# Holding the loads behind the fourth unit until the first 288 columns' low rank is copied

## The chip, the cores and the metric

The kernel runs on one core of one Trainium2 chip. A core has TensorE (PE, matmuls; its weight loads are listed apart as PEld), VectorE (DVE), ScalarE (ACT), GpSimd (POOL) and SyncE (SP), which issues the DMA transfers. The metric is the device time of one execution in microseconds, lower is better. Comparisons leave disturbed runs out.

## What is computed

Two parts, one behind the other. The first is a gated linear attention over 4 batches, 8 heads, 768 steps and head dimension 48:

```python
f = 1.0 / (1.0 + np.exp(-f_logit))
for t in range(S):
    state = f[:, :, t, :, None] * state + np.einsum('bhd,bhe->bhde', k[:, :, t], v[:, :, t])
    y[:, :, t] = np.einsum('bhd,bhde->bhe', q[:, :, t], state)
```

Its output, with the heads side by side, is x, 768 x 384 for each batch. The second part mixes along the steps with a low rank of 32 and then along the channels with two weights, 384 x 1536 and 1536 x 384:

```python
xt = x.transpose(0, 2, 1)
h = xt @ U @ V
u = x + h.transpose(0, 2, 1)
ch = np.maximum(u @ w_ch1, 0.0) @ w_ch2
return u + ch
```

The four parameters U, V, w_ch1 and w_ch2 arrive as 8-byte floating-point numbers and are converted on the chip to 4-byte ones.

## The kernel before

A *unit* is one batch and one pair of heads, so there are 16 units, and units 0 to 3 are batch 0. Units 0 to 3 are worked off first, with nothing beside them. Then the low rank of batch 0 is formed, first for the 288 columns of units 0 to 2 and then for the last 96, and the channel matmuls of batch 0 run while units 4 to 7 are worked off, and so on.

Operands of even units come into the tile `late`, those of odd units into `other`, one third each for f, k and q; v has three buffers of its own. So unit 5 takes the places of unit 3 in `other`, and v of unit 5 the buffer of unit 2. `load` issues them on SP, two DMAs (two heads) each for f, k and q and three for v:

```python
    def load(n, *names):

        b, hp = divmod(n, HP)
        for nm in names:
            if nm == "v":
                v_tiles[n] = three.tile([P, NBL, 2, D], F32, name="v_nat")
            for par in range(2):
                head = src[nm][b, 2 * hp + par]
        ...
                if nm == "v" or n < TURNED:
                    dst = v_tiles[n] if nm == "v" else nat[n % 2][nm]
                    nc.sync.dma_start(out=dst[:, :, par, 0:D], in_=head.rearrange("(c p) d -> p c d", p=P))
                    continue
```

A weight is taken in by two calls. `start` gives it a staging buffer and issues its DMA; `end` converts it: two instructions on ScalarE (L90, L91), three on VectorE, one on GpSimd (L95):

```python
        def start():
            raw = pool.tile([P, WP], U64, name="w_raw", bufs=RAW) if place is None else place()
            raw = T["raw"] = raw[0:rows, 0:n]
            dma.dma_start(out=shaped(raw), in_=w)

        def end():
            y = pool.tile([P, WP], U32, name="w_y")[0:rows, 0:n]
            r = pool.tile([P, WP], I32, name="w_r", bufs=3)[0:rows, 0:n]
            words = T["raw"].bitcast(U32).rearrange("p (n two) -> p n two", two=2)
            lo, hi = words[:, :, 0], words[:, :, 1]

            f = y.bitcast(F32)
            nc.scalar.activation(f, hi.bitcast(F32), AF.Abs)
            nc.scalar.activation(r, lo, AF.Copy, scale=2.0**-29)
            nc.vector.tensor_scalar(f, f, SMALLEST, LARGEST, ALU.max, ALU.min)
            nc.vector.tensor_scalar(y, y, 3, 0x3FFFFFFF, ALU.logical_shift_left, ALU.bitwise_and)
            nc.vector.scalar_tensor_tensor(y, hi, 0xC0000000, y, ALU.bitwise_and, ALU.bitwise_or)
            nc.gpsimd.tensor_tensor(dst.bitcast(I32), shaped(y.bitcast(I32)), shaped(r), ALU.add)

        return start, end


def ahead_by(n, loads):


    def call(i):
        if i + n < len(loads):
            loads[i + n][0]()
        loads[i][1]()

    return [lambda i=i: call(i) for i in range(len(loads))]
```

U and V (three pieces) and the later pieces are staged in a pool of four buffers (`w_raw`); the first six pieces of w_ch1 (128 of its 1536 columns each) in halves of `zw` tiles, which have another use only later:

```python
    spare = []

    def place():
        if not spare:
            t = zp.tile([P, NFC // 2, 2 * P], F32, name="zw").rearrange("p i t -> p (i t)").bitcast(U64)
            spare.extend([t[:, 0:WP], t[:, WP : 2 * WP]])
        return spare.pop(0)

    FIRST = 6
    weights += [
        take_in(w1[:, :, i * P : (i + 1) * P], w1_rows[:, :, i * P : (i + 1) * P], place if i < FIRST else None)
        for i in range(NFC)
    ]
```

The framework orders the instructions of TensorE, VectorE and ScalarE as the program has them (`manual_schedule`). The DMA issues of SP and the work of GpSimd are ordered by the framework itself; it adds all waits, for data and for places that are still being read.

The first four units, the loads for the next two, and the start of the mixer:

```python
        for n in range(HP):
            pieces = front(n, "keep", "keys") + rear(n - 1, "scan", "scores")
            pieces += [lambda: busy(3)] + rear(n, "kept") + front(n, "read_back", "queries")
            if n + 1 < HP:
                pieces += front(n + 1, "gates") + rear(n - 1, "read", "inner") + rear(n, "states")
            for piece in pieces:
                piece()
            if n < 2:
                load(n + 2, "v")
            if n == 1:


                for start, _ in weights[: early + 2]:
                    start()
            elif n > 1:
                load(n + 2, "f", "k", "q", "v")
        for start, _ in weights[early + 2 : early + FIRST]:
            start()


        loads = ahead_by(early + FIRST, weights)
        done, rest = slice(0, 2 * n * D), slice(2 * n * D, DM)
        pieces = rear(n, "states") + rear(n - 1, "read") + rear(n, "scan") + loads[:1] + rear(n, "scores")
        pieces += loads[1:2] + rear(n - 1, "inner") + rear(n, "read") + loads[2 : early + 1]
        for piece in pieces:
            piece()
        m = mixer(0)
        low_rank_of, added_up_of, mix_of = m.some
        low_rank_of(done)
        loads[early + 1]()
        for piece in rear(HP - 1, "inner"):
            piece()
        added_up_of(done)
        low_rank_of(rest)
        mix_of(done)
        added_up_of(rest)
        mix_of(rest)
        loads = loads[early + 2 :]

        start = m.before[3:5] + m.firsts[0:1] + m.before[5:]

        EARLY = 6
        second = chain(front(HP, "gates", "keep", "keys", "read_back", "queries"), steps(HP, 2 * HP + 1))
        for i, (_, piece) in enumerate(start + m.firsts[1:]):
            piece()
            if loads:
                loads.pop(0)()
            if i >= EARLY:
                next(second)()
        for f in loads:
            f()
```

The low rank of some columns ends with a copy on ScalarE (L213), on which the next matmul waits:

```python
        def low_rank_of(cols):
            pm = ps_big.tile([P, 2, 512], F32, name="ph", tag="big")[:, 0]
            for c in range(NCH):
                g = slice((c % NG) * R, (c % NG + 1) * R)
                nc.tensor.matmul(pm[g, cols], lhsT=U[:, c, :], rhs=x[:, c, cols],
                                 start=(c < NG), stop=(c >= NCH - NG))
            if not hs:
                for i in range(2):
                    hs[i] = two.tile([P, DM], F32, name="h", bufs=2)
            nc.scalar.copy(hs[0][:, cols], pm[:, cols])

        def added_up_of(cols):
            pm = ps_big.tile([P, 2, 512], F32, name="ph", tag="big")[:, 0]
            nc.tensor.matmul(pm[:, cols], lhsT=blocks, rhs=hs[0][:, cols], start=True, stop=True)
            nc.scalar.copy(hs[1][:, cols], pm[:, cols])
```

The loop over `start + m.firsts` gives, in this order, the turn of the first pair of row blocks (transposes on TensorE, a copy to `uT` on ScalarE), the turn of the second, the first channel matmuls of pair 0 (12 matmuls and a relu on ScalarE, L258 and L268), the turn of the third, the channel matmuls of pairs 1 and 2, and so on; behind each of these one weight is converted.

Of the kernel before, what the change touches and what calls it, by code (L numbers as in the profile page):

```python
# [10 lines left out]
F32 = mybir.dt.float32  # L11
U32 = mybir.dt.uint32
U64 = mybir.dt.uint64
# [5 lines left out]
WP = 384  # L19

RAW = 4
# [80 lines left out]
# [9 lines that stand above are left out]
# [362 lines left out]
def factored_path(ctx, tc, q, k, v, f_logit, moe_U, moe_V, moe_w_ch1, moe_w_ch2, out, ok):  # L473
# [4 lines left out]
    nc = tc.nc  # L478
    B, H, S, D = q.shape
    P = nc.NUM_PARTITIONS  # L480
# [4 lines left out]
    HP = H // 2  # L485
# [4 lines left out]
    NFC = FF // P  # L490
# [17 lines left out]
    zp = ctx.enter_context(tc.tile_pool(name="zp", bufs=3))  # L508
# [9 lines left out]
    raw = [{nm: t[:, i, :] for i, nm in enumerate("fkq")} for t in (late, other)]  # L518
# [11 lines left out]
# [8 lines that stand above are left out]
                if nm == "v" and par:  # L538

                    for s in range(2):  # L540
                        nc.sync.dma_start(
                            out=v_tiles[n][(1 - s) * C : (2 - s) * C, :, par, :],
                            in_=head.rearrange("(c s p) d -> s p c d", s=2, p=C)[s],
# [6 lines that stand above are left out]
                head = head.rearrange("(c i) d -> i c d", i=NB)  # L550
                for part in range(2):
                    p0 = par * PAD + part * NB
                    n_ch = min(NB, D - part * NB)
                    nc.sync.dma_start(
                        out=raw[n % 2][nm][p0 : p0 + NB, :].rearrange("p (c d) -> p c d", d=NB)[:, :, 0:n_ch],
                        in_=head[:, :, part * NB : part * NB + n_ch],
                    )
# [43 lines left out]
    table = one.tile([P, 1], F32, name="table")  # L601
# [7 lines left out]
    weights = [take_in(U, moe_U.rearrange("(c p) r -> p c r", p=P))]  # L609
    weights += [take_in(*pair) for pair in by_rows(V, moe_V, R)]  # L610
    early = len(weights)
    w1_rows = moe_w_ch1.rearrange("(c p) f -> p c f", p=P)

    spare = []

    def place():
        if not spare:
            t = zp.tile([P, NFC // 2, 2 * P], F32, name="zw").rearrange("p i t -> p (i t)").bitcast(U64)
            spare.extend([t[:, 0:WP], t[:, WP : 2 * WP]])
        return spare.pop(0)  # L620

    FIRST = 6
    weights += [
        take_in(w1[:, :, i * P : (i + 1) * P], w1_rows[:, :, i * P : (i + 1) * P], place if i < FIRST else None)
        for i in range(NFC)
# [96 lines left out]
    def mixer(b):  # L722
        return Mixer(tc, b, x_tiles[b], U, V, w1, w2, sums if b else None, ident, blocks, out, two, three, zp, ps_big, ps_mm,
                     b == 0, z_all, room if b >= B - 2 else None, FEWER - (b - B + 2) * NCH // 4)
# [172 lines left out]
    def front(n, *names):  # L897

        if n >= NU:
            return []  # L900
        if n not in ahead:
            ahead[n] = dict(zip(("gates", "keep", "keys", "read_back", "queries"), prepare(n)))
        return [ahead[n].pop(nm) for nm in names]

    def rear(n, *names):

        if not 0 <= n < NU:
            return []
        if n not in here:
            here[n] = dict(zip(("kept", "states", "scan", "scores", "read", "inner"), attend(n)))  # L910
        return [here[n].pop(nm) for nm in names if nm in here[n]]

    def steps(first, last):


        for n in range(first, last):
            yield from rear(n - 1, "scores") + rear(n, "kept") + front(n + 1, "gates", "keep", "keys")
            yield from rear(n - 1, "read")
            made = rear(n, "states", "scan")
            yield lambda: [f() for f in made]  # L920
            yield from front(n + 1, "read_back", "queries") + rear(n - 1, "inner")
            if n + 2 < NU:
                load(n + 2, "v")

    def attention(pieces, portions, todo):

        fill = Fill(todo, portions)
        for piece in pieces:
            fill()
            piece()  # L930
        fill.rest()

    def beside(pieces, n, calls):

        for i, piece in enumerate(pieces):
            yield piece
            for f in calls[:2] if i >= n else []:
                calls.remove(f)
                f()
        assert not calls  # L940

    def start_mixer(b, after):

        m = mixer(b)
        n = len(after) // 4
        pieces = after[:n] + m.before[:1] + after[n : 2 * n] + m.before[1:2] + after[2 * n : 3 * n]
        pieces += m.before[2:3] + after[3 * n :] + m.before[3:]
        for _, piece in pieces:
            piece()
        return m  # L950
# [4 lines left out]
    with tc.manual_schedule(engines={nc.vector.engine, nc.scalar.engine}):  # L955


        idle = ps_mm.tile([P, 512], F32, name="idle", tag="mm")

        def busy(n):  # L960
            for _ in range(n):
                nc.tensor.matmul(idle[:, 0:DM], lhsT=ident, rhs=ends[:, 0:DM], start=True, stop=True)  # L962

        busy(1)
        for piece in front(0, "gates"):
# [12 lines that stand above are left out]

                for start, _ in weights[: early + 2]:
                    start()  # L980
            elif n > 1:
                load(n + 2, "f", "k", "q", "v")
        for start, _ in weights[early + 2 : early + FIRST]:
            start()


        loads = ahead_by(early + FIRST, weights)
        done, rest = slice(0, 2 * n * D), slice(2 * n * D, DM)
        pieces = rear(n, "states") + rear(n - 1, "read") + rear(n, "scan") + loads[:1] + rear(n, "scores")
        pieces += loads[1:2] + rear(n - 1, "inner") + rear(n, "read") + loads[2 : early + 1]  # L990
        for piece in pieces:
            piece()
        m = mixer(0)
        low_rank_of, added_up_of, mix_of = m.some
        low_rank_of(done)
        loads[early + 1]()
        for piece in rear(HP - 1, "inner"):
            piece()
        added_up_of(done)
        low_rank_of(rest)  # L1000
        mix_of(done)
        added_up_of(rest)
        mix_of(rest)
        loads = loads[early + 2 :]

        start = m.before[3:5] + m.firsts[0:1] + m.before[5:]

# [10 lines that stand above are left out]
        n = len(m.seconds) // (NBL // 2)  # L1018
        todo, after = m.seconds[:-n], m.seconds[-n:]

        attention(second, 12 + 10 * HP - (len(start) + len(m.firsts) - 1 - EARLY), todo)
        m = start_mixer(1, after)
        for f in to_sum:
            f()
# [5 lines left out]
    pieces = beside(steps((B - 1) * HP + 1, NU + 1), 10 * (HP - 2), [lambda i=i: sum_of_w(i) for i in range(len(W_SUMS))])  # L1030
# [374 lines left out]
```

## Time and profile before

| | |
|---|---|
| time | 489.45 us, median of 3 runs (487.82 to 489.92) |
| profiled run | 488.68 us, span of the core 486.9 us |
| TensorE busy | 469.2 us, 96% of the span |
| VectorE busy | 355.4 us, 73% |
| ScalarE busy | 163.2 us, 34% |
| GpSimd busy | 37.6 us, 8% |
| chain that ended last | PE 79%, DVE 10%, DMA 3%, "issue" 3%, ACT 2% |
| moved by DMA | 34.34 MB, mean 71 GB/s |
| from 44 to 50 us | TensorE busy 3.67 of 6.00 us, DMA share 0.92 |
| from 50 to 56 us | TensorE busy 4.63 of 6.00 us, DMA share 0.96 |
| from 56 to 66 us | TensorE busy 10.00 of 10.00 us, DMA share 0.92 |

The busy time of an engine is a mean over stages with different limits, so the page's 40 slices and the timeline of single stretches say more than the sums. The chain that ended last follows the work back from the last instruction, at each step to what released it. "issue" in it is time in which an engine waited for nothing that the profile shows. A time in brackets behind an instruction is how long its engine stood idle before it, and for what. The DMA share is the mean busy share of the core's 16 DMA engines, counted over data and instructions alike.

### The profile page before, as it was taken

What the parts mean: (1) busy time and instruction counts of PE and PEld (TensorE: products, weight loads), DVE (VectorE), ACT (ScalarE), POOL (GpSimd) and SP (SyncE); (2) the same over time, 40 slices, a digit from 0 to 9 for tenths busy, and PEclk for the clock granted to TensorE, in tenths of its full rate; (3) what the DMA queues carried; (4) which work ended last, traced back from release to release, by engine and by line L of the source; (5) the groups of instructions that cost most, each with busy time, mean ns of one, the idle gap of its engine ahead of it and who ended that gap; (6) DMA issues with size and microseconds to landing.
All of it is one profiled execution on the core that took longest, in us unless ns stands there. A gap on an engine that the chain in (4) does not pass through costs nothing.

```text
span 486.9 us, 12734 instructions
## 1 busy us (share of the span) xinstructions
PE 469.2 (96%) x5541; PEld 400.0 (82%) x5541; DVE 355.4 (73%) x563; ACT 163.2 (34%) x309; POOL 37.6 (8%) x49
## 2 busy tenths in 40 slices
PE   7996899999999999999999999999999999999995
PEld 4775688886566568899898888899979999999995
DVE  5887689777999857656857548797896886958642
ACT  2444666664334313423231403433231312112200
POOL 3002245453000000000000000000000000000000
PEclk9999999999999999999999999999999999999999
DMA  9979975756778512333535100100000000000001
GB/s 146 158 153 178 254 194 135 162 143 79 110 116 121 96 41 36 52 48 67 76 55 94 25 18 18 27 3 20 19 1 1 33 2 18 16 1 34 1 33 38
DMA packets 158679, 34.34 MB, mean 71 GB/s; under 512 B 149206, under 2 KB 157078, under 8 KB 158614
## 3 DMA queue, kind: packets, MB, share of 16 engines
q1 hardware_dynamic: 158614, 33.44, 37.0%
q8 instruction: 45, 0.74, 0.6%
q14 instruction: 20, 0.16, 0.1%
HBM read 28.70 MB, written 4.72 MB: 69 GB/s over the span
## 4 chain that ended last, share of the span: by engine, by line
PE 79%; DVE 10%; DMA 3%; issue 3%; ACT 2%; SPq 2%; DVEq 0%; ACTq 0%
PE pw L312 26%; PE pz L258 23%; PE pp L410 11%; PE y L863 2%; PE pt L660 2%; PE sc L788 2%; PE ds L825 2%; PE y L881 2%; PE po L283 2%; PE idle L962 2%; PE put L246 1%; DMA late<-in_f_logit_dram 1%; DVE late L694 1%; DVE late L712 1%; PE pt L809 1%
## 5 line engine op out<-in xcount | busy, mean ns | idle before, releaser
L258 PE MATMUL pz<-uT,w 128*128 128x256 f32 x504 | 115.7, 383 | 0.3 <-ACT uT L247 0.3
L258 PEld LDWEIGHTS pz<-uT,w 128*128 128x128 f32 x504 | 93.4, 190 | 13.3 <-issue 0.5
L312 PE MATMUL pw<-w,z_all 128*128 128x192 f32 x216 | 37.7, 329 | 0.0
L312 PE MATMUL pw<-zw,w_raw 128*128 128x192 f32 x216 | 37.4, 327 | 0.0
L312 PEld LDWEIGHTS pw<-zw,w_raw 128*128 128x128 f32 x216 | 35.2, 190 | 0.8 <-issue 0.6
L312 PEld LDWEIGHTS pw<-w,z_all 128*128 128x128 f32 x216 | 35.0, 190 | 0.7
L95 POOL TENSOR_TENSOR w<-w_y,w_r 128x384 int32<-128x384 int32 x24 | 31.5, 1311 | 41.5 <-DVE w_y L94 36.5
L694 DVE TENSOR_TENSOR_SCAN late<-fz,late 128x768 f32<-128x768 f32 x16 | 28.1, 1755 | 8.9 <-ACT fz L689 4.2
L268 ACT ACTIVATE z_all<-pz 128x512 f32<-128x512 f32 x33 | 19.7, 596 | 41.4 <-PE pz L258 41.3
L410 PE MATMUL pp<-v_nat,late 128*128 128x128 f32 x224 | 28.8, 275 | 0.0
L712 DVE TENSOR_TENSOR_SCAN late<-fz,other 128x768 f32<-128x768 f32 x16 | 27.9, 1745 | 0.1
L410 PEld LDWEIGHTS pp<-v_nat,late 128*128 128x128 f32 x224 | 27.0, 192 | 0.0
L283 PE MATMUL po<-w,zw 128*128 128x384 f32 x72 | 25.6, 499 | 0.0
L283 PE MATMUL po<-w,z_all 128*128 128x384 f32 x72 | 25.3, 496 | 0.3 <-DVE o L187 0.3
L403 ACT ACTIVATE other<-other 128x512 f32<-128x512 f32 x18 | 11.3, 631 | 39.9 <-DVE other L187 39.9
L851 ACT COPY st<-added 128x576 f32<-128x576 f32 x12 | 14.7, 1224 | 27.5 <-DVE added L846 27.5
L92 DVE TENSOR_SCALAR w_y<-w_y 128x384 f32<-128x384 f32 (+3 forms) x27 | 13.1, 485 | 14.0 <-ACT w_y L90 13.8
L795 DVE TENSOR_TENSOR A<-sc,causal 128x768 f32<-128x768 f32 x16 | 15.2, 947 | 10.7 <-PE sc L788 10.7
L283 PEld LDWEIGHTS po<-w,z_all 128*128 128x128 f32 x72 | 13.1, 190 | 8.7 <-DVE o L187 0.9
L283 PEld LDWEIGHTS po<-w,zw 128*128 128x128 f32 x72 | 12.9, 189 | 8.7 <-issue 1.2
L187 DVE TENSOR_TENSOR w_raw<-z_all 128x768 f32<-128x768 f32 x12 | 11.4, 954 | 10.6 <-ACT z_all L268 9.2
L312 PE MATMUL pw<-w,other 128*128 128x192 f32 x108 | 18.6, 327 | 0.0
(193 smaller groups left out, 825.6 us busy)
## 6 DMA issues: line engine op xcount, KB each, us to landing
w_raw<-in_moe_w_ch_dram SPq DMA_DIRECT2D x18, 384.0 KB, 3.9
out_dram<-o SPq DMA_DIRECT2D x24, 192.0 KB, 1.9
v_nat<-in_v_dram SPq DMA_DIRECT2D x16, 144.0 KB, 3.6
v_nat<-in_v_dram SPq DMA_DIRECT2D x32, 72.0 KB, 3.3
zw<-in_moe_w_ch_dram SPq DMA_DIRECT2D x6, 384.0 KB, 5.7
late<-in_f_logit_dram SPq DMA_DIRECT2D x10, 96.0 KB, 3.1
late<-in_k_dram SPq DMA_DIRECT2D x10, 96.0 KB, 3.0
late<-in_q_dram SPq DMA_DIRECT2D x10, 96.0 KB, 2.6
```

What stands on the lines that cost most here:

```text
L92: nc.vector.tensor_scalar(f, f, SMALLEST, LARGEST, ALU.max, ALU.min)
L95: nc.gpsimd.tensor_tensor(dst.bitcast(I32), shaped(y.bitcast(I32)), shaped(r), ALU.add)
L187: nc.vector.tensor_tensor(*args)
L258: nc.tensor.matmul(pm[:, i * 2 * P : (i + 1) * 2 * P], lhsT=w1[:, m, o : o + P], rhs=uT[a][:, m, :], start=(m == 0), stop=(m == NDC - 1))
L268: nc.scalar.activation(z[a, c][:, k : k + 2, :].rearrange("p i t -> p (i t)"), pm, AF.Relu)
L283: nc.tensor.matmul(pm, lhsT=z[a, i // NI][:, i % NI, s * P : (s + 1) * P], rhs=w2[:, i, :], start=(i == 0), stop=(i == NFC - 1))
L312: nc.tensor.matmul(pm[:, n * HM : (n + 1) * HM], lhsT=lhs[:, i, :], rhs=rhs[:, i, :], start=(i == 0), stop=(i == NI - 1))
L410: nc.tensor.matmul(pm[:, i, r * P : (r + 1) * P], lhsT=room["w"](wn)[:, r * P : (r + 1) * P], rhs=x_node(a, xn), start=((xn, wn) == of[0]) ...
L694: nc.vector.tensor_tensor_scan(backwards(X, S - 1, S), backwards(f, S, S), backwards(ends, S - 1, S), 0.0, ALU.mult, ALU.add,)
L712: nc.vector.tensor_tensor_scan(Y, f[:, 0:S], starts, 0.0, ALU.mult, ALU.add)
L795: nc.vector.tensor_tensor(T["A"], sc[:, :, 0 : NBL * C].rearrange("p h (c i) -> p h c i", i=C), causal.unsqueeze(1).unsqueeze(1).broadcast ...
L851: nc.scalar.copy(st, states.rearrange(by_e, c=NCH))
```

## The change

It puts the loads behind those of unit 4 later: those of unit 5's operands, of pieces 2 to 5 of w_ch1, and of pieces 6 to 9. In the program they now stand behind the low rank of the first 288 columns. As the framework orders SP's issues itself, two places are *held* as well: the first column of the staging place of w_ch1's piece 2 and the first column of unit 5's f. ScalarE reads both right behind the copy of the low rank, into a scratch column, so that no load may write there before. For the first of these reads there has to be something in the place, so GpSimd writes zeros into its column at the start; and the three `zw` tiles are taken at the start. The aim is that during the end of the fourth unit and the first low rank no transfers run beside TensorE. The number of weights in flight ahead of their conversion (`ahead_by`) is set to match.

```diff
--- before.py
+++ after.py
@@ -613,13 +613,18 @@
 
     spare = []
 
+    FIRST = 6
+    for _ in range(FIRST // 2):
+        t = zp.tile([P, NFC // 2, 2 * P], F32, name="zw").rearrange("p i t -> p (i t)")
+        spare.extend([t[:, 0 : 2 * WP], t[:, 2 * WP : 4 * WP]])
+
+
+    held = [spare[2][:, 0:1], raw[1]["f"][:, 0:1]]
+    nc.gpsimd.memset(held[0], 0.0)
+
     def place():
-        if not spare:
-            t = zp.tile([P, NFC // 2, 2 * P], F32, name="zw").rearrange("p i t -> p (i t)").bitcast(U64)
-            spare.extend([t[:, 0:WP], t[:, WP : 2 * WP]])
-        return spare.pop(0)
-
-    FIRST = 6
+        return spare.pop(0).bitcast(U64)
+
     weights += [
         take_in(w1[:, :, i * P : (i + 1) * P], w1_rows[:, :, i * P : (i + 1) * P], place if i < FIRST else None)
         for i in range(NFC)
@@ -978,22 +983,28 @@
 
                 for start, _ in weights[: early + 2]:
                     start()
-            elif n > 1:
+            elif n < HP - 1:
                 load(n + 2, "f", "k", "q", "v")
-        for start, _ in weights[early + 2 : early + FIRST]:
-            start()
-
-
-        loads = ahead_by(early + FIRST, weights)
+
+
         done, rest = slice(0, 2 * n * D), slice(2 * n * D, DM)
-        pieces = rear(n, "states") + rear(n - 1, "read") + rear(n, "scan") + loads[:1] + rear(n, "scores")
-        pieces += loads[1:2] + rear(n - 1, "inner") + rear(n, "read") + loads[2 : early + 1]
+        ends_of = [end for _, end in weights]
+        pieces = rear(n, "states") + rear(n - 1, "read") + rear(n, "scan") + ends_of[:1] + rear(n, "scores")
+        pieces += ends_of[1:2] + rear(n - 1, "inner") + rear(n, "read") + ends_of[2 : early + 1]
         for piece in pieces:
             piece()
         m = mixer(0)
         low_rank_of, added_up_of, mix_of = m.some
         low_rank_of(done)
-        loads[early + 1]()
+
+        for t in held:
+            nc.scalar.copy(table, t)
+        for start, _ in weights[early + 2 : early + FIRST]:
+            start()
+        load(n + 2, "f", "k", "q", "v")
+        for start, _ in weights[early + FIRST : early + FIRST + RAW]:
+            start()
+        ends_of[early + 1]()
         for piece in rear(HP - 1, "inner"):
             piece()
         added_up_of(done)
@@ -1001,7 +1012,7 @@
         mix_of(done)
         added_up_of(rest)
         mix_of(rest)
-        loads = loads[early + 2 :]
+        loads = ahead_by(FIRST - 2 + RAW, weights[early + 2 :])
 
         start = m.before[3:5] + m.firsts[0:1] + m.before[5:]
```

## The prediction, made before the changed kernel ran

> **What bounds the kernel now.** I read the page's busy shares first, then the chain that ended last, then the same stretch engine by engine, then the SP queue. In 40 slices of 12.2 us the page says of TensorE and of the DMA engines:
>
> ```profile
> PE   7996899999999999999999999999999999999995
> DMA  9979975756778512333535100100000000000001
> q8 instruction: 45, 0.74, 0.6%
> ```
>
> TensorE is at 9 in all but a few slices, so this kernel is bound by TensorE, and time can be won only where TensorE waits. The weakest inner slice is the fourth (36.5 to 48.7 us): the end of the first four units, where DMA is at 9 too. TensorE's own timeline there:
>
> ```profile
> 42.13 0.74 PE L788 MATMUL sc<-qT,kz 48*64 48x64 f32 x34 [1.72 <-issue]
> 42.66 0.90 PE L881 MATMUL y<-v_nat,A 64*64 64x48 f32 x48
> 43.34 1.22 PE L863 MATMUL y<-st,qT 48*64 48x48 f32 x44
> 44.49 0.43 PE L208 MATMUL ph<-x,U 128*32 128x288 f32 x1
> 46.86 1.16 PE L208 MATMUL ph<-x,U 128*32 128x288 f32 x11 [1.94 <-issue]
> ```
>
> The reader is to see two holes in brackets, 1.72 and 1.94 us, released by "issue": no engine and no data transfer released them, and both stand inside a run of equal matmuls. Between them lie 34+48+44+1 = 127 matmuls, with as many weight loads 254 instructions. That is a block of instructions that had not arrived. The transfers of the queue of instructions (45 in all) fit: in the trace one runs from 39.32 to 40.54 and TensorE goes on at 42.13; the next from 44.12 to 45.51 and it goes on at 46.86. Both holes are on the chain of waits. So is what follows; the chain again (start, us, engine, tile, line):
>
> ```profile
> 48.06 0.02 ACT h L213
> ...
> 48.35 0.56 ACT w_y L90
> 48.92 0.44 ACT w_r L91
> 49.36 0.54 ACT x L887
> ```
>
> From 48.06 to 50.19 ScalarE has no gap, and TensorE waits for it. From 55.84 to 113 us TensorE is busy throughout (33.00 of 33.00 us from 80 to 113), so a delay before that is kept. The SP queue in these microseconds (start, us in which it issues, and what, xcount):
>
> ```profile
> 43.80 2.14 SPq L548 DMA_DIRECT2D other<-in_f_logit_dram  x2
> 46.04 1.35 SPq L548 DMA_DIRECT2D other<-in_k_dram  x2
> 47.49 2.44 SPq L548 DMA_DIRECT2D other<-in_q_dram  x2
> 49.98 1.20 SPq L81 DMA_DIRECT2D zw<-in_moe_w_ch_dram  x2
> 51.27 0.43 SPq L548 DMA_DIRECT2D v_nat<-in_v_dram  x1
> 51.76 1.54 SPq L541 DMA_DIRECT2D v_nat<-in_v_dram  x2
> 53.34 1.98 SPq L81 DMA_DIRECT2D zw<-in_moe_w_ch_dram  x2
> ```
>
> Unit 5's f, k and q come first, then w1 pieces 2 and 3, unit 5's v, then pieces 4 and 5. Note that v stands *before* the weights in the program: it had no free buffer yet and was overtaken. Unit 6's v (57.94) likewise goes ahead of unit 6's f (68.21), which stands earlier in the program. **So the SP queue isn't in the order of the program: what is free to go overtakes what isn't.**
>
> **The skill.** "Runtime: NRT & Kernel Launch", section "Instruction fetch mechanics", says that instructions come in blocks of 16 KiB, 256 instructions, over a DMA queue of the sequencer's own. The trace agrees: 0.74 MB in 45 transfers is 16.4 KB each, and the holes are 254 recorded instructions apart. "DMA: Bandwidth & Descriptors", section "Queues, rings and completion order", says that a DMA engine takes its queues in turn, so a fetch waits behind data packets; the time from the restart at 42.13 to the fetch's start at 44.12 agrees, though no run here shows an idle fetch.
>
> **The change part by part.**
>
> 1. *Two reads on ScalarE* right behind the copy of the low rank (48.06). A like copy of two columns ("seen") is recorded at 0.16 us, and its successor starts 0.06 us after it (44.61, 44.67). Two cost 0.1 to 0.3 us, on the gapless stretch above, so on the path: **+0.2 us**. The memset on GpSimd is early and beside everything.
>
> 2. *What the gate holds.* A load waits only if it writes bytes that the two reads touch: w1 piece 2 (the first column of its place) and the two heads of unit 5's f. Pieces 3, 4, 5 and unit 5's k and q write other bytes. By what the SP queue shows, they are not held by the program's order: at 43.80 they are free and go. I expect from 43.80: w1 3, 4, 5, then k and q, w1 piece 6 (its staging buffer is free), v, and only then piece 2, f, pieces 7 to 9.
>
> 3. *The two holes.* The first (1.72) ends before 43.80, where nothing differs yet: unchanged. For the second, the fetch starts at 44.12, when loads issued from 43.80 have moved next to nothing (f of 43.80 lands at 47.61, the v before it at 47.05). At most its own 1.38 us and the 1.35 us behind it get shorter, towards the 0.92 us of the fetch at 33.32: **0 to -0.5 us** with an empty queue, 0 with the leak of step 2.
>
> 4. *Piece 2 becomes late.* Landing events of the trace: the last load before 43.80 lands at 47.05; w1 pieces land 1.3 to 1.4 us apart when in a row (54.47, 55.85; 62.70, 63.75, 65.16, 66.43), heads of f some 0.9 to 1.5 us apart. Ahead of piece 2 now stand 3 pieces (4.2), 4 heads (3.6), piece 6 (1.4), v (1.7), then itself (1.4): 47.05 + 12.3 = 59.4 us, instead of 54.47. Its conversion is next on ScalarE after the first turn's copy, at 55.59 before. ScalarE takes its work in order: from 59.4 it does piece 2 (1.0), the second turn's copy (0.7), piece 3 (1.0), a relu (0.6), piece 4 (1.0), the third turn's copy (0.75): 64.4 us. TensorE began the matmuls that need this last copy at about 61.8 (two groups of 12, 2.65 us each, before the end at 67.1). So TensorE waits some **2.6 us**, and as it is full afterwards, most of it stays: say **+2.2 us**.
>
> 5. *Unit 5's operands later.* Its gates are about six pieces of the second stage after unit 4's at 66.94, near 100 us; f lands near 61. Hidden. Later staged pieces (7 to 9) land near 62 to 65, used at 65.0 to 70.9. Hidden.
>
> Sum with the leak: +0.2 + 2.2 = +2.4 us, on about 489.2 (between the median 489.45 and the profiled 488.68): **491.6 us**.
>
> **Rivals.** *A: the gate is tight*: all of w1 2 to 5, f, k and q stay behind the reads, as the title of the change wants. Then SP issues only v from 43.80 and the weights at about 48.6, 1.4 us before 49.98. Pieces 2 to 5 land at about 52 to 56, earlier than now; six heads (5.1 us) put piece 6 at about 62.9 against 62.70 now. Nothing is late, the second hole shrinks by up to 0.5 or, if the fetch suffers more from the traffic than I read, by its whole 1.94 us. With the +0.2 that makes -0.3 to -1.7: 487.5 to 489 us. For it: the gate stands where the holes are, and with the two reads it is aimed at just these loads. Against it: v and unit 6's v in the trace, and that five of seven groups of loads share no byte with the gate.
>
> *B: the transfers become the bound for longer.* With a tight gate the DMA engines rest from about 47 to 50 us, and they are full till 67 (DMA share 0.92 from 56 to 66). Piece 6 is used at 63.00 and landed at 62.70: there is 0.3 us of room. If heads go slower than I took them, ScalarE waits for pieces 6 and 7 and holds relu copies back: up to +1.5 us, 489 to 491 us.
>
> *C: all is hidden.* ScalarE has idle time for it from 58 us on (0.53, 1.09, 1.00 us before relus) and two PSUM buffers stand between it and TensorE. Then only +0.2 remains: 489.4 us. Against it: DVE is at 9.23 of 10 us from 56 to 66, ScalarE at 8.35, so little can be made up there.
>
> **Range and chances.** I give the leak 0.65, the tight gate (with or without B) 0.25, C 0.1. 0.65 x 491.6 + 0.25 x 488.6 + 0.1 x 489.4 = 490.6 us. The range runs from the tight gate with half of its gain, 488.0, to the leak with piece 2 landing 1.5 us later than reckoned, 493.2. Two per cent are 9.8 us; all that the change touches lies between 43.8 and 67 us, and no case above reaches half of that. Hence 0.01 faster, 0.97 within, 0.02 slower.
>
> **What would show it.** In the SP queue of the changed kernel, behind v of unit 4 at about 43.8: zw loads at once (leak) or none until about 48.5 (tight). In TensorE's timeline: the 1.72 us hole unchanged; the 1.94 us one within 0.5. On ScalarE: two copies of one column after the low-rank copy, 0.1 to 0.3 us in the row. In step 4: a gap before the conversion of piece 2 that the DMA releases, near 56 to 59 us, and TensorE waiting for uT or z_all copies before 67 us. The prediction is wrong if the second hole closes (traffic that I hold for harmless was delaying the fetch), if the first changes too, or if the weights come in an order that I haven't thought of, so that a piece other than 2 is the late one.

## The result, and the profile after

The changed kernel takes **503.19 us** (median of 4 runs, 502.12 to 504.41) against 489.0 for the kernel before: a ratio of 1.0292, 95% interval 1.0258 to 1.0326. It is slower by 14.2 us, and the prediction, 490.6 us in a range from 488.0 to 493.2, was wrong.

From the page of the changed kernel, the slices of TensorE, its clock and the DMA engines, the data queue, and one group of instructions (busy us, mean ns, then idle time before it and what ended it):

```profile
PE   7579699999999999999999999999999999999995
PEclk9859879999999999999999999999999999999999
DMA  9999783667477742331633410000000000000001
q1 hardware_dynamic: 164902, 34.62, 38.0%
L665 PE MATMUL pt<-ident,late 128*128 128x128 f32 x54 | 10.3, 343 | 9.7 <-DMA late<-in_f_logit_dram 9.4
```

Two of these lines on the page of the kernel before, the clock and the data queue:

```profile
PEclk9999999999999999999999999999999999999999
q1 hardware_dynamic: 158614, 33.44, 37.0%
```

Three things are new, and none lies where the prediction looked. TensorE's weak slices begin with the *second* (12.6 to 25 us), not with the fourth. The granted clock, at 9 throughout before, falls to 5. And the queue moved 34.62 MB where the page before says 33.44: **1.18 MB more, though the change was to move loads, not to add any**. One unit's f, k, q and v are 8 x 144 KB = 1.18 MB. The group of transposes waited 9.4 us for f in `late`.

TensorE's timeline shows the wait, SP's timeline who is behind it (start, us, what, xcount):

```profile
18.46 0.87 PE L665 MATMUL pt<-ident,other 128*128 128x128 f32 x6
28.46 1.51 PE L665 MATMUL pt<-ident,late 128*128 128x128 f32 x6 [9.13 <-DMA late<-in_f_logit_dram]
```

```profile
14.06 1.13 SPq L548 DMA_DIRECT2D late<-in_f_logit_dram  x2
...
22.37 1.52 SPq L541 DMA_DIRECT2D v_nat<-in_v_dram  x2
23.93 1.20 SPq L548 DMA_DIRECT2D late<-in_f_logit_dram  x2
25.18 1.13 SPq L548 DMA_DIRECT2D late<-in_k_dram  x2
26.36 1.64 SPq L548 DMA_DIRECT2D late<-in_q_dram  x2
```

Unit 2's f is loaded at 14.06 and once more at 23.93, into the same place. In the kernel before, the same transposes began at 20.02:

```profile
20.02 0.85 PE L660 MATMUL pt<-ident,late 128*128 128x128 f32 x6 [0.53 <-DMA late<-in_f_logit_dram]
```

They take 1.51 us instead of 0.85: that is the clock, which is 0.50 in the trace from 21.05 to 38.11 us.

The cause stands in the diff. Before, the loads behind the first four units were under `if n == 1 ... elif n > 1`, so units 2 and 3 (n) loaded units 4 and 5. Now they are under `if n == 1 ... elif n < HP - 1`. That takes away n = 3, as was meant, and lets **n = 0** in: `load(2, ...)` runs a second time, after the first unit's operations have already loaded unit 2.

TensorE stands 8.4 us behind the kernel before at these transposes (28.46 against 20.02), 11.5 at the first matmul of the low rank (56.02 against 44.49), 15.4 at the first channel matmuls (71.22 against 55.84), and 15.8 at the end of the span (502.7 against 486.9). (The profiled run is the slowest of the four, 504.41 us, so these distances are somewhat larger than the 14.2 us of the medians.) So nearly all is lost before 72 us, and nothing is given back. The two holes that the change was aimed at are still there, the second one larger:

```profile
53.67 0.73 PE L793 MATMUL sc<-qT,kz 48*64 48x64 f32 x33 [1.25 <-issue]
...
59.48 2.13 PE L208 MATMUL ph<-x,U 128*32 128x288 f32 x10 [2.79 <-issue]
```

### The profile page after: what moved, and what is told of

Read it like the earlier page. It is cut to its first block, busy times and chain, and to the rows that moved or that the text cites. A ratio compares the mean times of both kernels' runs of the same rounds, so it can differ in the third digit from the quotient of the medians.

```text
span 502.7 us, 12743 instructions
## 1 busy us (share of the span) xinstructions
PE 476.8 (95%) x5541; PEld 405.9 (81%) x5541; DVE 355.6 (71%) x563; ACT 163.6 (33%) x311; POOL 37.5 (7%) x50
## 3 DMA queue, kind: packets, MB, share of 16 engines
q1 hardware_dynamic: 164902, 34.62, 38.0%
## 4 chain that ended last, share of the span: by engine, by line
PE 75%; DVE 12%; DMA 5%; issue 3%; SPq 2%; ACT 2%; DVEq 0%; ACTq 0%
PE pw L312 25%; PE pz L258 19%; PE pp L410 11%; PE pt L665 2%; PE y L886 2%; PE y L868 2%; PE sc L793 2%; PE idle L967 2%; PE ds L830 2%; PE put L246 2%; DVE late L717 2%; PE po L283 2%; DVE late L699 1%; PE pt L814 1%; SPq L548 1%
## 5 line engine op out<-in xcount | busy, mean ns | idle before, releaser
L886 PEld LDWEIGHTS y<-v_nat,A 64*64 64x64 f32 x768 | 14.0, 145 | 7.1 <-issue 3.7
L665 PE MATMUL pt<-ident,late 128*128 128x128 f32 x54 | 10.3, 343 | 9.7 <-DMA late<-in_f_logit_dram 9.4
```

The source lines that it names most:

```text
L665: nc.tensor.transpose(pt[:, 2 * c // NBL, c % (NBL // 2) * P : (c % (NBL // 2) + 1) * P], nat[n % 2][nm][:, c].rearrange("p h d -> p (h d) ...
L886: nc.tensor.matmul(o(s, par, c), lhsT=T["A"][part[s ^ par], par, c, :], rhs=vt[part[s ^ par], c, par, :], start=False, stop=True, skip_gro ...
```

## The experiments

Theory 1: the second load of unit 2 is the whole loss. Theory 2: the gate and its leak (step 4 of the prediction) are, only larger than reckoned. None of the runs leaves out a part of the computation. Ratios are to the kernel before, run on the same chip.

### The changed kernel without the second load

```diff
-            elif n < HP - 1:
+            elif 1 < n < HP - 1:
```

> The changed kernel with the condition of the loads written so that the first unit's turn (n = 0) no longer loads unit 2 a second time; gate and order of the weights as in the change. Theory 1 (the second load of unit 2's f makes TensorE wait 9.13 us at 19.3 us, and the lower clock behind it costs the rest): the wait and the lower clock are gone, time 488 to 492 us. Theory 2 (the gate and the late w1 piece 2 cost the time, as step 4 of the prediction had it, only more of it): the time stays above 498 us. My old sum for this kernel was 491.6 us.

Measured: 490.42 us, ratio 1.0047 (1.0026 to 1.0068). Theory 2 is out. This is the kernel whose time I had reckoned, 491.6 with the leak and 490.6 weighted, so the steps about the gate can be read here. SP's timeline, and ScalarE's:

```profile
42.89 2.65 SPq L81 DMA_DIRECT2D zw<-in_moe_w_ch_dram  x3
45.58 0.49 SPq L548 DMA_DIRECT2D other<-in_f_logit_dram  x1
46.17 2.88 SPq L548 DMA_DIRECT2D other<-in_k_dram  x2
...
53.59 0.53 SPq L81 DMA_DIRECT2D zw<-in_moe_w_ch_dram  x1
```

```profile
46.95 0.19 ACT L1001 COPY table<-zw 128x1 f32<-128x1 f32 x1
47.18 0.19 ACT L1001 COPY table<-other 128x1 f32<-128x1 f32 x1
...
57.63 0.56 ACT L90 ACTIVATE w_y<-zw 128x384 f32<-128x384 f32 x1 [2.26 <-DMA zw<-in_moe_w_ch_dram]
```

The gate leaks as foretold: three weight pieces at once at 42.89, even one of the two heads of f (the column read lies in the first head only), and piece 2 alone at 53.59. ScalarE then waits 2.26 us for piece 2, and TensorE 0.38 and 0.27 us for `uT` copies behind it.

### The second load alone

```diff
+            elif n == 0:
+                load(2, "f", "k", "q", "v")
             elif n > 1:
```

This is added to the kernel before.

> The kernel before with one thing added: unit 2's f, k, q and v are loaded a second time after the first unit. No gate, the order of all other loads as before. Theory 1: 500 to 504 us, a wait of about 9 us for f of unit 2 near 19 us, and a mean granted clock of 0.97 to 0.98. Theory 2: 489 to 493 us, the 1.18 MB more are hidden behind the compute.

Measured: 499.93 us, ratio 1.0228 (1.0195 to 1.026), 0.1 us under the range of theory 1. The clock, 0.982 to 0.986 in its four runs, was a little above the 0.97 to 0.98 that were expected. TensorE waits for f of unit 2:

```profile
28.26 1.51 PE L660 MATMUL pt<-ident,late 128*128 128x128 f32 x6 [9.17 <-DMA late<-in_f_logit_dram]
```

So the second load costs 10.97 us by itself, the rest of the change 1.46 in the run above; together 12.4 of the 14.2. The other 1.8 us are not settled. They lie within the intervals (by the ratios, 1.0292 against 1.0228 and 1.0047, 0.8 us are left), and they go along with a lower clock: 0.972 to 0.982 in the four runs of the changed kernel. In its profiled run the clock falls a second time (mean 0.67 from 62 to 72 us), which the second load alone does not show in its profile (1.00 from 50 to 75 us). Nor need the two costs simply add: the changed kernel's timeline has no wait of TensorE for piece 2, because TensorE comes there late.

### Which of the four tiles

```diff
-                load(2, "f", "k", "q", "v")
+                load(2, "k", "q", "v")
```

> The kernel before with only k, q and v of unit 2 loaded a second time, f once. Which load of the four makes the wait? If it is the place that f needs at the head of unit 2 (theory 1 as I read the chain): no wait at f, but k of unit 2 lands again near 27 to 28 us where its transposes stood at 23.8, so a wait of 2 to 5 us, time 491 to 496 us. If it is the bytes alone, whichever load carries them: three quarters of the loss, 498 to 501 us.

Measured: 495.75 us, ratio 1.0124 (1.0088 to 1.0161), in the lower range. f holds nothing up (TensorE waits 1.35 us and starts its transposes at 20.15, before at 20.02), and the wait goes to the next tile:

```profile
28.72 1.51 PE L660 MATMUL pt<-ident,late 128*128 128x128 f32 x6 [4.69 <-DMA late<-in_k_dram]
```

Then f alone:

```diff
-                load(2, "f", "k", "q", "v")
+                load(2, "f")
```

> The kernel before with f of unit 2 alone loaded a second time (0.29 MB of the 1.18 MB), behind v of unit 2 as in the change. Theory P (place: TensorE may read f only when the last writer of its place has landed): a wait for f of some 7 to 9 us from 19 us and a lower clock behind it, although few bytes are added: 495 to 500 us. Theory Q (bytes: 1.18 MB elsewhere cost 7.5 us, so a quarter of them costs a quarter): 490 to 491.5 us.

Measured: 501.66 us, ratio 1.0238 (1.0191 to 1.0285). A quarter of the bytes costs all of the loss. TensorE's timeline of this run:

```profile
28.64 1.51 PE L660 MATMUL pt<-ident,late 128*128 128x128 f32 x6 [9.25 <-DMA late<-in_f_logit_dram]
```

For this wait it is the place that counts, not the amount: a second writer of a tile that is due takes its position at the end of SP's queue, nine transfers behind the first one, and the reader waits for both. (501.66 lies somewhat over the predicted 500 at most, and its interval covers that of the full second load. In its profile the clock stays at 0.50 until 41.42 us, with the full second load until 36.51.)

### The same bytes to another place

```diff
+            elif n == 0:
+                flat = z_all.rearrange("p a t -> p (a t)")
+                # both heads of f, k, q, v of unit 2, written into flat: 8 DMAs of 144 KB
```

> The kernel before, with the same 1.18 MB of unit 2's f, k, q and v read a second time at the same point of the program, but written to a place that nothing reads until much later (z_all). Theory P (it is the place: f of unit 2 may be read only when its last writer has landed): no wait for f at 19 to 28 us; unit 3's k and q come 6 us later than before and cost 0 to 3 us; 489 to 493 us. Theory Q (it is the bytes and the queue time): as the second load alone, 498 to 501 us.

Measured: 496.44 us, ratio 1.0155 (1.013 to 1.0179): **neither theory**. I had thought these bytes nearly free. There is no wait for unit 2's f, but two others, both in TensorE's timeline:

```profile
37.50 1.51 PE L660 MATMUL pt<-ident,other 128*128 128x128 f32 x6 [4.56 <-DMA other<-in_k_dram]
...
65.96 0.80 PE L258 MATMUL pz<-uT,w 128*128 128x256 f32 x1 [2.98 <-ACT uT L247]
```

SP issued the eight transfers from 25.07 to 31.53, so everything behind came 6 to 9 us later: unit 3's k (issued at 31.63, before at 24.96), and w1 piece 2 (59.20, before 49.98), for which ScalarE waited 4.9 us and thereby held back `uT`. The two waits of TensorE come to 7.5 us, nearly the whole loss. So these transfers have only a few us of lead over their readers (unit 3's k about 2 us: 6.7 us later, 4.56 us waited). They are a second bound right under TensorE.

### How much of it is the clock

The clock was tested by giving TensorE work in the wait: 12 calls of the kernel's own dummy matmul right in front of unit 2's f, in the changed kernel and in the kernel with the second load alone.

```diff
-                pieces += front(n + 1, "gates") + ...
+                pieces += [lambda: busy(12)] * (n == 1) + front(n + 1, "gates") + ...
```

> The changed kernel as it is, with 12 more dummy matmuls (some 8.8 us of TensorE) right where it waits for unit 2's f, so that it is busy instead of idle in the 9.13 us. If part of the loss is the clock that fell to 0.60 to 0.78 after the wait (matmuls of 0.9 us took 1.5): the clock stays near 1.00 until 50 us, and the time falls from 503.2 to about 499 to 500 us. If the clock follows something else, such as the transfers: 503 us or more, as before.

Measured: 498.46 us, ratio 1.0234 (1.0176 to 1.0293), a median 4.7 us under the changed kernel's, though the intervals overlap: three of the four runs lie from 497.80 to 498.62, one at 505.14.

> The second load alone (499.9 us), with 12 dummy matmuls where TensorE waits for unit 2's f. If idle time lowers the clock and the clock then costs time by itself: transposes and matmuls from 28 us on take 0.9 us again and not 1.5, and the time falls by 2.5 to 4.5 us to 495.5 to 497.5 us, with the same wait for f. If most of what the fill gained in the changed kernel (4.7 us) came from the shifted instruction blocks and not from the clock: 498.5 us or more.

Measured: 497.21 us (median of the three undisturbed runs, 495.21 to 497.73), ratio 1.015 (1.0097 to 1.0203), 2.7 us under the second load alone, at the edge of what the intervals tell apart. The wait for f shrinks to what the dummies leave of it:

```profile
28.59 0.85 PE L660 MATMUL pt<-ident,late 128*128 128x128 f32 x6 [1.38 <-DMA late<-in_f_logit_dram]
```

The clock itself is plain. Busy time by stretch of the second load alone, and then of the same with the fill (PE, PEld, DVE, ACT, POOL, then clock, DMA share, GB/s):

```profile
19.00:29.00 10.00, 0.83 (x5) 0.77 (x5) 2.50 (x2) 0.49 (x1) 0.00 (x0) 0.69 0.99 167
29.00:42.00 13.00, 12.74 (x272) 10.45 (x270) 7.92 (x10) 4.76 (x10) 0.00 (x0) 0.71 0.99 147
```

```profile
19.00:29.00 10.00, 8.62 (x33) 5.12 (x32) 3.30 (x3) 1.29 (x2) 0.00 (x0) 1.00 1.01 166
29.00:42.00 13.00, 12.40 (x373) 10.06 (x372) 10.05 (x13) 5.91 (x13) 0.00 (x0) 1.00 0.93 146
```

The transfers are as busy in both and the wait for f ends at the same time (transposes at 28.59 with the fill, 28.26 without). With the fill the clock stays at 1.00, and TensorE gets 373 instead of 272 matmuls done in the next 13 us. So in this wait idleness lowers the clock, not traffic, and the lower clock costs some 2.7 us behind the wait. Not all of that is shown to be the clock: the added matmuls also move the borders of the instruction blocks.

The record has a second reading of it. The kernel before ran 77 times beside these experiments, with mean clocks from 0.987 to 1.000, and the time rises by 3.3 us for each 0.01 that the clock is lower (a straight line through the 77 runs, correlation -0.85). By that rate, an estimate, the runs with the second load alone (mean 0.984) lose some 4 us against those with the fill (0.996), and the changed kernel (0.978, outside the range of the 77) some 6 us against the kernel before (0.995). With the 8.4 us that TensorE is late at the transposes, 6 us come near the 14.2. It is a correlation, not an experiment, but it roughly agrees with both fills.

### A gate that holds what it was meant to hold

The first experiment again, with the gate on GpSimd (in outline): from the copied low rank it writes one column of each place concerned (pieces 2 to 5, both heads of unit 5's f, k and q, the staging buffers of pieces 6 to 9).

```diff
-        for t in held:
-            nc.scalar.copy(table, t)
+        for t in zws[1:]:
+            nc.gpsimd.tensor_copy(first column of both halves of t, hg[:, 0:2])
+        nc.gpsimd.tensor_copy(first column of all heads in other, hg[:, 0:6])
+        # and one column of each of four w_raw buffers, taken here for pieces 6 to 9
```

> The first experiment's kernel (no second load of unit 2) with a gate that holds all it was meant to hold: GpSimd, not ScalarE, writes one column of every place concerned (w1 pieces 2 to 5, both heads of unit 5's f, k and q, the four staging buffers of pieces 6 to 9) from the copied low rank, so that only v still goes ahead. Theory L (the leak makes piece 2 late, ScalarE waits 2.26 us for it and TensorE some 0.9 us in all): the wait is gone, piece 2 lands near 51 us, and the time is 0.5 to 1.5 us below the first experiment's 490.4: 488.9 to 489.9 us. Theory B of the prediction (full gate, transfers then late): ScalarE waits for pieces 6 to 9 instead, 490 to 492 us. The hole of 1.4 to 1.9 us at the second instruction block: within 0.5 us of before in both.

Measured: 489.15 us, ratio 1.0003 (0.9983 to 1.0022), 0.35 us over the kernel before, where the leaky gate was 1.46 over: 1.1 us better. Piece 2 is not waited for. ScalarE waits 1.55 us for a staged piece at 62.64 instead, as rival B said, but no wait of TensorE follows from that. The second hole is 1.39 us, 0.55 under that of before and so just outside the 0.5 expected.

The same without any gate, so with the new order in the program alone:

```diff
-        for t in held:
-            nc.scalar.copy(table, t)
```

> The first experiment's kernel without any gate: only the new order in the program remains (pieces 2 to 5 ahead of unit 5's f, k and q, pieces 6 to 9 behind). Theory L: piece 2 is no longer late (it goes at 43 us with the others), ScalarE doesn't wait, and the two reads are gone: 1.0 to 1.6 us under 490.4, so that of before within 0.5 us, 488.6 to 489.4. If the gate was doing good by quieting something: 490.4 or more.

Measured: 488.47 us, ratio 0.999 (0.9975 to 1.0006): a shade under the foretold range, and the same as before. So the 1.5 us of the first experiment come from its gate: the two reads on ScalarE, and piece 2 held back alone. A complete gate gains nothing over none.

### Unit 4's loads behind the gate too

```diff
-            elif 1 < n < HP - 1:
-                load(n + 2, "f", "k", "q", "v")
+        # behind the complete gate: pieces 2 to 5, unit 4, pieces 6 to 9, unit 5
```

> As the run with all held, and unit 4's f, k and q behind the gate too (in the order pieces 2 to 5, unit 4, pieces 6 to 9, unit 5). From about 39 to 46 us only v is then in flight. Theory T (TensorE's instruction blocks come late because data packets are ahead of them in the DMA engines): both holes, 1.72 and 1.94 us before, shrink to under 0.8 us each, and the time falls by 1.5 to 3 us under the run with all held. Theory I (a fetch takes its 4 to 5 us anyway and the block in between is too short): the holes keep 1.2 us or more each, and the time is that of the run with all held, or above it where unit 4 comes late.

Measured: 487.59 us, ratio 0.9981 (0.9968 to 0.9993). It is the only kernel here that beats the one before, by 0.9 us of 488.8 (0.3 to 1.6). The two holes at the instruction blocks:

```profile
42.52 0.74 PE L797 MATMUL sc<-qT,kz 48*64 48x64 f32 x34 [0.27 <-issue]
46.11 1.16 PE L208 MATMUL ph<-x,U 128*32 128x288 f32 x11 [0.74 <-issue]
```

They fall from 1.72 and 1.94 to 0.27 and 0.74 us, as theory T foretold, and 1.56 us by the medians under the run with all held lies at the low end of its range (the intervals of these two overlap). So a little of what the change was for can be had, if the loads of *unit 4* wait as well.

That the blocks come sooner because no data is in flight is not shown, and the trace speaks against it in part. From 41 to 45 us the DMA share was 0.05 in this run and 1.10 before. Yet the fetch in front of the second hole took 1.19 us (from 43.66), before 1.38 (from 44.12), and 0.96 (from 43.09) with all held, at a share above 1. In the kernel before itself, 21 of the 45 fetches run while the data queue moves nothing, and they take 0.92 to 1.39 us. So data in flight does not lengthen these fetches; what differs is that the second began sooner after TensorE had gone on, 1.14 us instead of 1.99. The fetch in front of the first hole was no quicker than before (39.81 to 41.08, before 39.32 to 40.54). TensorE came to that border 1.8 us later, after 3.4 us at a clock of 0.50 from 22.66 on, and so waited less. In the run with the bytes elsewhere, too, TensorE came there late, and stood at neither border although the DMA share was above 1.0 from 43 to 46 us. How early TensorE gets to the border is thus a rival that no run here excludes.

The holes also vary from run to run: the first measured 0.98, 0.71 and 0.44 us in three other kernels that differ nowhere in their loads before it. And the profile is of the slowest of this kernel's 22 runs (489.44 us). The gain in time, from 22 runs, is the firm part; its cause stays open.

## Why the prediction was wrong

- **The failed step is the first half of step 3, with the list of parts before it**: that the first hole "ends before 43.80, where nothing differs yet", and in "Range and chances" that "all that the change touches lies between 43.8 and 67 us". I had taken the new condition for "n = 3 no longer loads". It also means "n = 0 loads", and I never put in the four values of n. The range rested on that: no case in it had a load more.
- **Step 1** (two reads, +0.2 us): recorded at 0.19 us each, and what follows starts 0.62 us behind the low-rank copy instead of 0.29, so +0.33. Somewhat over.
- **Step 2** (the leak): right, save that one head of f goes free as well, and that piece 6 does not go ahead (pieces 6 to 9 are issued at 55.80, behind piece 2).
- **Step 3, the second hole** (0 to -0.5 us): 1.39 us without the second load, 2.79 in the changed kernel, against 1.94. The first agrees, within what varies from run to run. That the fetch was long because it waits behind data packets is not borne out: 1.22 and 1.38 us in front of the two holes, and 0.92 to 1.39 us for the 21 fetches of the same trace that have no data beside them. The prediction held that no run shows an idle fetch; they stand later in the very trace that it read.
- **Step 4** (piece 2 late, TensorE 2.6 us): the mechanism is right, the size was not. ScalarE waits 2.26 us, TensorE 0.65 for `uT` copies. The mis-sized term is the landing of piece 2: 59.4 in my sum, 57.55 in the first experiment. There the last load in front of the gate landed at 45.73 instead of 47.05, and piece 6 did not go ahead. From the landing on, ScalarE's row was as reckoned, 4.9 us to the end of the third turn's copy against 5.0. All in all +1.5 us was measured against the +2.4 of my sum, and not all of it is this wait: the reads of step 1 are in it, and in the profiled run a stretch at a clock of 0.50 from 51.92 to 55.33 us. That 490.42 lies so near the weighted 490.6 is luck, as that figure is a mean over cases.
- **Step 5** (later operands are hidden): no wait for unit 5's operands in the first experiment.
- **Rival A** (tight gate, a gain of 0.3 to 1.7 us) gained nothing, 1.0003; the second hole was 1.39 us with the complete gate and 1.74 with none. Only with unit 4 held too was there a gain, of 0.9 us.
- What no step had: the clock. "TensorE: Matmul & The Clock Gate" in the Trainium skill, section "What's actually happening", states that the array runs at half its clock after about 3.4 us of idleness. The trace agrees with the half: a mean of 0.60 from 19 to 29 us is 2 us at full clock and 8 at half. It does not agree with the time: the half clock begins 1.7 us into the wait in the changed kernel, 3.8 with the second load alone, and 5.0 with the second f. I had looked for waits of TensorE and not asked what they do to the matmuls behind them.

## What to carry to other kernels

When a change rewrites a condition, put in every value of the loop variable before anything is reckoned, and compare the bytes that the program moves: 1.18 MB more on the page would have told it at once. In a queue as full as this one, a transfer costs by its position: a second writer of a tile that is due makes the reader wait for its own turn in the queue, and bytes to elsewhere still push back everything behind them. A gate made by touching bytes holds only the transfers that write those bytes; list them one by one.

## What the runs showed of the hardware

- A wait of 9 us leaves TensorE at a lower clock well after it works again: in the changed kernel the mean is 0.65 from 29 to 42 us, and transposes take 1.51 us there instead of 0.85. The half clock ends at 38.11 us, 9.7 us after TensorE is busy again; 8.3 us with the second load alone, 12.8 with the second f. Dummy matmuls in the wait kept the clock at 1.00 (twice).
- A block of instructions that comes late costs between nothing and 2.8 us of TensorE at one place of the program, from kernel to kernel and from run to run. In the one profile with unit 4's loads held as well, it was 0.27 and 0.74 us. Fetching a block took 0.92 to 1.39 us where no data moved (21 times in the kernel before), so the transfers beside it do not explain the 1.22 and 1.38 us in front of the two holes.
- Reading 1.18 MB to a place that nobody waits for cost 7.6 us of 489, although the data queue took only 37% of the DMA engines' time over the whole span of the kernel before. What counts is the first 66 us, where the kernel before has a mean DMA share of 0.82 from 21 to 40 us and of 0.92 or more in the stretches around it.
